# Attention's steps written out as one order of their own for each unit

## The chip, the cores and the metric

The kernel runs on one core of a Trainium2 chip. Its engines are TensorE (PE, matrix products), VectorE (DVE), ScalarE (ACT), GpSimd (POOL) and SyncE (SP), which here issues most DMAs. Each works through its own instructions in the order in which they were issued, and waits on semaphores for the others. The metric is the device time of one execution in microseconds.

## What is computed

A transformer block with adaptive layer norm: attention with a compressive memory over four segments of 512 rows, 32 heads of 18, then a SwiGLU feed-forward part.

```python
def _A_ref(x, wq, wk, wv, wo, beta):
    q, k, v = ...                              # (B, H, N=4, L=512, Dh=18)
    for s in range(N):
        logits = einsum("bhqd,bhkd->bhqk", q[:, :, s], k[:, :, s]) * scale + mask
        a_dot = softmax(logits) @ v[:, :, s]
        pq = phi(q[:, :, s])                   # phi(t) = t + 1 if t > 0 else exp(t)
        a_mem = (pq @ M) / (pq @ z + 1e-6)
        o[s] = g * a_mem + (1 - g) * a_dot     # g = sigmoid(beta)
        pk = phi(k[:, :, s]);  M = M + pk.T @ v[:, :, s];  z = z + pk.sum()
    return o @ wo
...
h = layernorm(x) * (1 + ca) + sa;  x = x + ga * A(h)
h = layernorm(x) * (1 + cb) + sb;  x = x + gb * ((silu(h @ w_gate) * (h @ w_up)) @ w_down)
```

## The kernel before

Three parts follow each other: the projections of segments 0 to 2 (up to some 217 us), attention, and the feed-forward part, whose products are formed by a Strassen-like scheme from sums of blocks of the normed rows (`y`). The change is in attention alone.

Attention is cut into 32 **units**: unit u is segment u // 8 and four heads. In a unit, 12 **score steps** `a` are taken. One score step issues, on PE, the products for one PSUM bank of two kinds and what follows them: for unit u + 2 the logits by rows, `p1_step` (L175), from which DVE takes the row maxima (`junk`, L190); for unit u the logits by columns with the maxima taken off, `p2_step` (L662), from which ACT makes the exponentials `Pt` (L668); POOL then masks the diagonal part (L672). Each kind has three banks. Widths go down from 512 to 128 columns within a unit. Between score steps stand the other steps, each a letter in a table; a digit is a quarter, half or block:

- `V`: the products of unit u - 1's `Pt` with v (`av`, L685, 32 matmuls); `E`: ACT copies them out (L697); `c`: PE transposes them (L706, four matmuls); `d`: DVE divides by the row sums and scales (L714, L715, L722), and POOL adds to the output rows (L723)
- `m`: PE transposes unit u + 1's row maxima (L205); `n`: ACT copies them (L209) and SP sends them by two DMAs into the operand `qs` (L164), where unit u + 1's column products need them
- `M`, `X`: a part of the output projection of an earlier segment (L785, 14 matmuls in four quarters M0 to M3) and the sum with x on DVE (L790); in units 1 to 7 it is segment 3's v projection (L862) instead. `R`, `S`, `T` prepare its left operand: PE transposes, ACT copy, DVE remainder (L759, L765, L769); `Z`, `z` the same for its last columns
- `A`, `B`, `C`, `D`, `G`: the memory part, on PE (L921), ACT, POOL, DVE and POOL; `f`, `h`: loads of phi(q) for it (`pq`, L909), with a POOL memset
- `P`, `Q`, `q`, `Y`: load of a block of wo (L1037), multiply on POOL (L1041), cast on ACT (L1043), remainder on DVE (L1045)
- `l`, `p`, `x`: layer norm of finished rows on DVE, POOL, ACT, with a store; `W`: segment 3's q and k projection, in unit 0

From unit 17 on, two helpers (`stage_a`, `stage_b`) also prepare the feed-forward operands `y`: a load, PE transposes, ACT scaling, then for each operand an ACT cast, a DVE remainder and a store, with POOL differences in between.

The order is that of the Python code (`tc.manual_schedule`). It is set by the table `PAT`: five patterns of 11 places, one for unit 0 and four chosen by the half of the segment and the parity of u, so units with the same pattern have the same order. Next unit's loads (`load_unit(u + 3)`) come at a unit's start, a segment's v loads after place 5, and the `y` steps at places worked out from `KP` and collected in `sched`.

```python
PAT = (("a a Q D", "a G V0123 m E q", "", "a a", "a M0 M1", "n a a c Y M2 d M3 X", "", "a a", "h f a R P Z S T", "", "z a"),
```

Of the kernel before, what the change touches and what calls it, by code (L numbers as in the profile page):

```python
# [42 lines left out]
DS = 4  # L43
DP = (5, 6)
PM = ()
KP = (9, 7, 10, 9)
WW = (11, 15, 18, 22, 27)
SS = (2, 3, 4, 5, 25, 27)
HH = (4, 6, 8, 16, 20, 24)
# [8 lines left out]
WQ = (1, 3, 4, 5, 6)  # L58
E1 = 3
E2 = 2  # L60
PAT = (("a a Q D", "a G V0123 m E q", "", "a a", "a M0 M1", "n a a c Y M2 d M3 X", "", "a a", "h f a R P Z S T", "", "z a"),
# [4 lines left out]
LNA = 1  # L66
S3 = (4, 5, 6, 7, 8, 0, 1, 2, 3)
S1B, S2B, XB = 3, 3, 2
# [8 lines left out]
def block(ctx: ExitStack, tc: tile.TileContext, x, wqk, wv, wo, beta, wgu, wd, c, w_mod, wm01, out):  # L77
# [652 lines left out]
        nc.sync.dma_start(vq[s][:, j, :], vD[s][:, j, :])  # L730

    yt = {}

    def yh(k, kb):
        return yt[1][:, k - 1, kb] if k else yt[0][kb]
# [231 lines left out]
    def event(ev, u):  # L967
        n, a = ev[0], ev[1:]
        s, q = divmod(u, 8)
        if n == "W":  # L970
            seg3_step(int(a))
        elif n == "L":
            load_unit(4)
        elif n == "V":
            for j in a:
                av_step(u - 1, int(j))
        elif n == "E":
            ev_step(u - 1)
        elif n == "m":
            if (NE < u + 1 < NU) or u == 0:  # L980
                mt_a(max(u + 1, NE), ps, *(("x", XB) if u else ("s1", S1B)))
        elif n == "n":
            if (NE < u + 1 < NU) or u == 0:
                mt_b(max(u + 1, NE))
        elif n == "c":
            comb_a(u - 1)
        elif n == "d":
            comb_b(u - 1)
        elif n == "f" and s < 3 and q < 4 and u:
            if u == 1:  # L990
                phi_q(1, 0)
                phi_q(1, 1)
            phi_q(s + 1, q + 1)
        elif n == "h" and s < 3 and q == 0 and u:
            phi_q(s + 1, 0)
        elif n in "DG" and u > 0:
            s1, q1 = divmod(u - 1, 8)
            if n == "G" and u < 9:
                v_st(u - 1)
            if s1 < 3 and q1 >= 4:  # L1000
                (num_d if n == "D" else num_e)(s1 + 1, q1 - 4, fq[-3])
        elif n in "ABC" and s < 3 and 4 <= q < 8:
            if n == "A":
                num_a(s + 1, q - 4, int(a))
            elif n == "B":
                num_b(s + 1, q - 4, int(a))
            else:
                fq[-3] = num_c(s + 1, q - 4)
        elif n in "Zz" and 1 <= s < 4 and q == 0:
            (wo_z if n == "Z" else wo_z2)(s - 1)  # L1010
        elif n in "RST" and 1 <= s < 4 and q % 2 == 0:
            (wo_r if n == "R" else wo_s if n == "S" else wo_t)(s - 1, q // 2)
        elif n in "MX":
            w = u - 9
            if 0 < u < 8:
                if n == "M":
                    v_m(u, int(a))
                else:
                    v_x(u)
            elif w >= 0 and w < 24:  # L1020
                si, h = divmod(w, 2)
                if n == "M":
                    wo_m(si // 4, si % 4, h, int(a))
                else:
                    wo_x(si // 4, si % 4, h)
        elif n in "lpx":
            w = (u - 9) | 1 if u % 2 == 0 else u - 10
            if 0 <= w < 23:
                if n == "l":
                    ln_a(w // 8, w % 8 // 2)  # L1030
                elif n == "p":
                    ln_b()
                else:
                    ln_c()
        elif n == "P" and s == 0 and q in WQ:
            fq[-1] = wk.tile([P, D], F32, tag="woraw", name="woraw", bufs=1)
            nc.sync.dma_start(fq[-1], wo[:, WQ.index(q), :])  # L1037
        elif n in "QqY" and s == 0 and q - 1 in WQ:
            k = WQ.index(q - 1)
            if n == "Q":  # L1040
                nc.gpsimd.tensor_tensor(fq[-1], fq[-1], gaB, op=ALU.mult)  # L1041
            elif n == "q":
                nc.scalar.copy(woh[:, k], fq[-1])  # L1043
            else:
                nc.vector.tensor_tensor(wol[:, k], fq[-1], f32(woh[:, k]), op=ALU.subtract)  # L1045
# [8 lines left out]
    sched = {}  # L1054

    def at(g, f):
        sched.setdefault(g, []).append(f)

    def y_lo(o, kb, f, st, c):
        if kb < 2:  # L1060
# [7 lines left out]
        else:  # L1068
            nc.sync.dma_start(yD[0][o][:96, 4, c], f32(st[:96, 0]))

    def y_part(g, o, kb, f, stf, hv, d=2):
# [7 lines left out]
        at(g, hi)  # L1079
        at(g + 1, lambda: y_lo(o, kb, f, box[0], c))  # L1080
        at(g + 1 + d, lambda: y_store(o, kb, box[0], c))

    def load_cols(dst, s, i0, kh, kb):
        c0 = 288 * kh + 128 * kb
# [13 lines left out]
        for i in range(4):  # L1098
            nc.tensor.transpose(pt[:n, i, :], xb[:, i, :n], ident)

    def step_of(u):
        return 11 * u + KP[u % 8 // 4 * 2 + u % 2]

    def flat(a):
        return a.rearrange("p a b -> p (a b)")

    def stage_a():
# [6 lines left out]
        pts = {}  # L1114
        for i in range(6):
            kb, kh = divmod(i, 2)
            u = 18 + i
            n = P if kb < 2 else 96
            h = yh(kh, kb)
            at(11 * (u - 1) + 1 if i else 11 * u, lambda i=i, kh=kh, kb=kb: load_cols(xb[i % 2], 0, 0, kh, kb))  # L1120
            g = step_of(u) if i else 11 * u + 10
            at(g, lambda i=i, n=n: trans4(xb[i % 2], n, pts, i))
            at(g + 1, lambda i=i, h=h, kh=kh, kb=kb: scaled(h, flat(pts.pop(i)), kh, kb))
            for hv in range(2):
                y_part(g + 2 + 3 * hv, kh, kb, h[:, 256 * hv:256 * hv + 256], lambda j=2 * i + hv: st[j % 4], hv)

    def stage_b():
        big = flat(sk2.tile([P, 5, L], F32, tag="pq", name="yq"))
# [11 lines left out]

        for i in range(6):
            hv, kb = divmod(i, 3)
            u = 25 + i
# [4 lines left out]
            at(11 * (u - 1) + 1, lambda i=i, hv=hv, kb=kb: load(i, hv, kb))  # L1148
            g = step_of(u)

            def trans(i=i, n=n):
                trans4(xb[i % 2], n, pts, i)
# [5 lines left out]

            def sub2(d, x, y_, op=ALU.subtract):
                nc.gpsimd.tensor_tensor(d, x, y_, op=op)  # L1160
            at(g, trans)
            at(g + 1, sc)
            at(g + 2, lambda b=b, h11=h11, a=a, n=n: sub2(b[:n], h11, a[:n]))
            at(g + 3, lambda h00=h00, a=a, n=n: sub2(h00, a[:n], h00))
            y_part(g + 6, 3, kb, h00, lambda i=i: sto[i % 2], hv)
            at(g + 5, lambda h01=h01, h11=h11: sub2(h01, h01, h11))
            at(g + 7, lambda h00=h00, h01=h01: sub2(h01, h01, h00, ALU.add))
            y_part(g + 4, 5, kb, b, lambda i=i: sts[i % 2], hv)

    def y_sum(kb):  # L1170
        n = P if kb < 2 else 96
# [329 lines left out]
    with tc.manual_schedule():  # L1501
# [2 lines left out]
        new_tmp3()  # L1504
        for j in range(4):
            load_v(0, j)
        for u in range(NU + 1):
            s, q = divmod(u, 8)
            if u > 1:
                load_unit(u + 3)  # L1510
            if u == 1:
                while s3q:
                    seg3_step(-1)
# [7 lines left out]
            ma, mb = [], []  # L1521
            ga = chain(*[p2_step(u, j, ma) for j in range(4)])
            gb = p1_seq(u + 2, mb)
            for k in range(11):
                if u == 17 and k == 0:
                    stage_a()
                if u == 24 and k == 0:
                    stage_b()
# [7 lines left out]
                if k == 5 and 4 <= q and s < 3:  # L1536
                    load_v(s + 1, q - 4)
            run(ga)
            run(gb)
        p2.close()  # L1540
        mid.close()
        ps = pool(p2r, "pst", 2, space=PSUM)
# [269 lines left out]
```

## Time and profile before

| | us |
|---|---|
| median of 3 runs | 1844.78 (1842.21 to 1845.96) |
| the profiled execution | 1846.91 |
| its span, first to last instruction | 1844.9 |
| attention's units 1 to 32 and the way to segment 3's output projection, in the span | 232.2 to 565.8 |

The profile's page gives, for one execution, each engine's busy time, and the chain of work that ended last, followed back from the last instruction. The trace behind it can be asked for a stretch of time: busy times by window, what each engine waited for, groups of like instructions, and single instructions in order of time. A matmul's end is modelled in it, so that PE's busy time also covers short holes.

### The profile page before, as it was taken

To read this page: it belongs to the slowest core of one execution; us is meant where nothing else is said; L and a number is where in the kernel's file an instruction comes from. 1 tells how busy PE (TensorE), PEld (TensorE's weight loads), DVE (VectorE), ACT (ScalarE), POOL (GpSimd) and SP (SyncE) were. 2 spreads that over 40 slices of the span, in tenths; PEclk is the share of its full clock that TensorE was granted. 3 is DMA by queue.
4 is the path that set the end of the run, shared out by engine and by line. 5 is a ranking of instruction groups with operands and counts; after the bars stand their busy time and mean duration, and the time that the engine had idled before them with its cause. 6 is when DMAs were issued, how large, how long until landed. Compare 5 with 4: busy or idle time off the path is not lost.

```text
span 1844.9 us, 31121 instructions
## 1 busy us (share of the span) xinstructions
PE 1815.5 (98%) x11061; PEld 1517.1 (82%) x11061; DVE 1491.5 (81%) x3309; ACT 955.7 (52%) x2137; POOL 494.4 (27%) x702
## 2 busy tenths in 40 slices
PE   8999999999999999999999999999999999999999
PEld 5888766666668888888888888888888888888888
DVE  7566578888977888988788898758888888888886
ACT  6444567667775454454445444434544544544541
POOL 2010146455562444446435443300000000000000
PEclk9999999999999999999999999999999999999999
DMA  8677755557648654554464444395333333324331
GB/s 290 234 236 272 244 158 158 159 158 219 175 132 295 227 171 157 191 187 154 153 210 146 147 158 154 122 301 156 123 105 104 102 106 119 102 90 128 105 102 52
DMA packets 178562, 304.49 MB, mean 165 GB/s; under 512 B 25304, under 2 KB 108184, under 8 KB 176616
## 3 DMA queue, kind: packets, MB, share of 16 engines
q1 hardware_dynamic: 151032, 248.66, 43.0%
q10 hardware_dynamic: 27376, 53.86, 8.3%
q8 instruction: 87, 1.43, 0.3%
q14 instruction: 67, 0.55, 0.1%
HBM read 188.42 MB, written 113.33 MB: 164 GB/s over the span
## 4 chain that ended last, share of the span: by engine, by line
PE 89%; DVE 5%; DMA 3%; issue 1%; ACT 1%; SPq 0%; POOL 0%; ACTq 0%; DVEq 0%
PE A L1339 24%; PE pd L1467 13%; PE C L1339 12%; PE pd L1448 10%; PE B L1339 6%; PE pp L524 4%; PE av L685 3%; PE pw L785 3%; PE pv L553 2%; PE s L662 2%; PE s L175 2%; PE pp L809 2%; DVE junk L190 1%; PE pm L513 1%; PE pn L921 1%
## 5 line engine op out<-in xcount | busy, mean ns | idle before, releaser
L1339 PE MATMUL A<-y,wh 128*128 128x512 f32 x1152 | 406.1, 393 | 1.5 <-ACT B L1385 1.0
L190 DVE CUSTOM_DVE_ANT_0 junk<-s,tri 128x384 bf16<-128x384 f32 (+3 forms) x512 | 221.9, 485 | 42.8 <-PE s L175 23.4
L1339 PEld LDWEIGHTS A<-y,wh 128*128 128x128 f32 x1152 | 216.7, 188 | 46.1 <-ACT B L1385 2.5
L1304 DVE TENSOR_TENSOR wl<-O,wh 128x256 fp32r<-128x256 f32 x504 | 248.7, 499 | 2.1 <-ACT wh L1303 1.6
L1339 PE MATMUL A<-y,wl 128*128 128x512 f32 x576 | 226.8, 394 | 0.0
L1453 DVE TENSOR_TENSOR acc<-acc,pd 128x576 f32<-128x576 f32 x216 | 162.0, 751 | 59.4 <-PE pd L1448 51.3
L1339 PE MATMUL C<-y,wh 128*128 128x512 f32 x576 | 203.0, 393 | 0.5 <-DVE cu L1362 0.5
L1303 ACT CAST wh<-O 128x256 fp32r<-128x256 f32 x504 | 197.5, 405 | 3.1 <-DMA yD<-st 3.1
L668 ACT ACTIVATE Pt<-s 128x512 f32<-128x512 f32 (+2 forms) x384 | 179.3, 529 | 35.4 <-PE s L175 22.5
L1467 PE MATMUL pd<-dh,ah 128*128 128x288 f32 x640 | 189.1, 295 | 0.5 <-DVE x L1471 0.5
L1467 PE MATMUL pd<-dh,al 128*128 128x288 f32 x640 | 189.2, 296 | 0.0
L1467 PE MATMUL pd<-dl,ah 128*128 128x288 f32 x640 | 188.9, 295 | 0.0
L1477 DVE TENSOR_TENSOR acc<-acc,pd 128x576 f32<-128x576 f32 x156 | 116.8, 749 | 87.1 <-PE pd L1467 86.6
L1294 POOL TENSOR_TENSOR O<-O 128x384 f32<-128x384 f32 x132 | 148.1, 1136 | 135.2 <-DMA O<-in_wgu_dram 61.7
L1408 ACT CAST ah<-sg 128x512 fp32r<-128x512 f32 x192 | 119.2, 621 | 74.8 <-DVE sg L1363 67.9
L1409 DVE TENSOR_TENSOR al<-sg,ah 128x512 fp32r<-128x512 f32 x192 | 137.2, 714 | 10.9 <-ACT ah L1408 10.8
L1448 PE MATMUL pd<-dh,ah 128*128 128x288 f32 x448 | 133.0, 297 | 0.0
L1448 PE MATMUL pd<-dh,al 128*128 128x288 f32 x448 | 132.5, 296 | 0.0
L1448 PE MATMUL pd<-dl,ah 128*128 128x288 f32 x448 | 132.4, 295 | 0.0
L1467 PEld LDWEIGHTS pd<-dh,ah 128*128 128x128 f32 x640 | 120.8, 189 | 6.8 <-DVE x L1471 0.8
L1467 PEld LDWEIGHTS pd<-dl,ah 128*128 128x128 f32 x640 | 120.5, 188 | 7.1
L1339 PEld LDWEIGHTS C<-y,wh 128*128 128x128 f32 x576 | 108.3, 188 | 21.3 <-DVE cu L1362 1.1
(410 smaller groups left out, 4353.6 us busy)
## 6 DMA issues: line engine op xcount, KB each, us to landing
O<-in_wgu_dram SPq DMA_DIRECT2D x36, 768.0 KB
O<-oD SPq DMA_DIRECT2D x36, 512.0 KB
oD<-O ACTq DMA_DIRECT2D x34, 512.0 KB
ks<-kD SPq DMA_DIRECT2D x64, 216.0 KB
qs<-qD SPq DMA_DIRECT2D x64, 216.0 KB
O<-in_wgu_dram SPq DMA_DIRECT2D x36, 384.0 KB
rD<-wr ACTq DMA_DIRECT2D x36, 336.0 KB
wr<-rD SPq DMA_DIRECT2D x35, 336.0 KB
```

Source lines behind the costliest of these rows:

```text
L190: nc.vector.tensor_tensor_reduce(junk[:, :n], bank[:, n * o:n * o + n], tri[:, L - n:], 1.0, -3e38, op0=ALU.add, op1=ALU.max, accum_out=mx ...
L668: nc.scalar.activation(pt[:, hs[0]:hs[-1] + 1:2, :n], bank[:, :n * per].rearrange("p (a b) -> p a b", a=per), AF.Exp, scale=SCALE)
L1294: eng.tensor_tensor(o[:, d], o[:, a], o[:, b], op=op)
L1303: nc.scalar.copy(wh, o)
L1304: later.append(lambda: nc.vector.tensor_tensor(wl, o, f32(wh), op=ALU.subtract))
L1339: nc.tensor.matmul(bank, lhsT=a, rhs=b, start=(first and n == 0), stop=(n == 6), skip_group_check=not first)
L1408: nc.scalar.copy(ah, src)
L1409: later.append(lambda: nc.vector.tensor_tensor(al, src, f32(ah), op=ALU.subtract))
L1448: nc.tensor.matmul(pd[:, i, :288], lhsT=a[:, tk], rhs=w, start=(k == 0), stop=(k == 2))
L1453: nc.vector.tensor_tensor(o, o, pd[:, :, :288], op=ALU.add)
L1467: nc.tensor.matmul(pd[:, i, :288], lhsT=a[:, tk], rhs=w, start=(k == 0), stop=(k == 5))
L1477: nc.vector.tensor_tensor(o, o, pd[:, :, :288], op=ALU.add)
```

## The change

`PAT`, `KP` and the planner `at`/`sched` go. In their place stands `ORDER`, a table with one line for each unit, in which every step is a token: also the loads of the next stack (`U`), of v (`v0` to `v3`), the start of the two helpers (`SA`, `SB`) and each single `y` step (`y0` to `y131`). A `<` or `>` ahead of a token does the step for the unit before or after, so steps can stand in a neighbour's line. Every step of before is there once; nothing is computed otherwise.

```diff
-PAT = (("a a Q D", "a G V0123 m E q", "", "a a", "a M0 M1", "n a a c Y M2 d M3 X", "", "a a", "h f a R P Z S T", "", "z a"),
...
+ORDER = (
...
+    "a a V0123 a a a G M0 E M1 a a a M2 a a P M3 c X a a >Q d",
...
+    "a a a V0123 <d E a a a m M0 n a a a c <f d M1 a a a M2 M3 R >U X",
...
-        for u in range(NU + 1):
-            s, q = divmod(u, 8)
-            if u > 1:
-                load_unit(u + 3)
...
-            for k in range(11):
...
-                for ev in PAT[q // 4 * 2 + u % 2 if u else 4][k].split():
-                    if ev == "a":
-                        scores(ga, gb, ma, mb)
-                    else:
-                        event(ev, u)
-                for f in sched.pop(11 * u + k, ()):
-                    f()
...
+        def act(tok, u):
+            nonlocal w3, o3, opl_, woh, wol
+            if tok[0] in "<>":
+                act(tok[1:], u + (1 if tok[0] == ">" else -1))
+            elif tok == "a":
+                step_a(u)
+            elif tok == "U":
+                load_unit(u + 3)
...
+            elif tok[0] == "y":
+                parts[int(tok[1:])]()
...
+            else:
+                event(tok, u)
+
+        for u, line in enumerate(ORDER):
+            for tok in line.split():
+                act(tok, u)
```

Three places show what this does to the engines' order. The line numbers of the changed kernel are some 29 higher.

SP, end of unit 0 and unit 1: `kD` is the store of segment 3's k, `pq` the loads of phi(q), `woraw` the load of a block of wo, `vt` a store of segment 3's v. Before:

```order
L288 DMA kD_94<-tmpa 128x2x512
L289 DMA kD_94<-tmpa 128x512
L909 DMA pq_2838<-qF_96 64x512
L909 DMA pq_2838<-qF_96 128x512 x2
L1037 DMA woraw<-in_wo_dram 128x576
```

And now:

```order
L317 DMA kD_94<-tmpa 128x2x512
L318 DMA kD_94<-tmpa 128x512
L901 DMA vD_102<-vt 128x304
L1065 DMA woraw<-in_wo_dram 128x576
L188 DMA ks_987<-kD_91 54x2x512
```

The load of wo has moved ahead of the three phi(q) loads, which follow seven rows later.

DVE, start of unit 10, whose row maxima are those of unit 12 (512 wide at first): PE's `V` of this unit stands behind its third score step, in both orders. Before:

```order
L714 RECIPROCAL r_4359<-px 128x16
L715 TENSOR_TENSOR r_4359<-r_4359,omg 128x16
L722 TENSOR_TENSOR tmp<-px,r_4359 128x288
L190 ISA junk,mx<-s_4373,tri 128x512
L190 ISA mx 128x1
L190 ISA junk,mx<-s_4380,tri 128x512
L190 ISA mx 128x1
L190 ISA junk,mx<-s_4387,tri 128x512
L190 ISA mx 128x1
L190 ISA junk,mx<-s_4415,tri 128x512
```

And now:

```order
L219 ISA junk,mx<-s_4366,tri 128x512
L219 ISA mx 128x1
L219 ISA junk,mx<-s_4373,tri 128x512
L219 ISA mx 128x1
L219 ISA junk,mx<-s_4380,tri 128x512
L219 ISA mx 128x1
L743 RECIPROCAL r_4403<-px 128x16
L744 TENSOR_TENSOR r_4403<-r_4403,omg 128x16
L751 TENSOR_TENSOR tmp<-px,r_4403 128x288
L219 ISA junk,mx<-s_4412,tri 128x512
```

Step d has moved from ahead of the first maximum to behind the third.

PE, the end of attention: `av` is the last unit's V, `pw` the matmuls of M, `px` step c, `pto` the first transposes of segment 3's output projection. Before, from the last score step:

```order
L662 MATMUL s_8614<-qs_2341,ks_2342 128x128 x2
L685 MATMUL av<-Pt,vq_6422 32x512 x4
L685 MATMUL av<-Pt,vq_6422 32x384 x4
L685 MATMUL av<-Pt,vq_6422 32x256 x4
L685 MATMUL av<-Pt,vq_6422 32x128 x4
L785 MATMUL pw<-woh,hh 128x288
```

There, seven `pw` rows stand between `av` and `px`, and seven between `px` and `pto`. Now, from the last of the `pw` rows, all 14 of which stand between the last score step and `av`:

```order
L815 MATMUL pw<-wol,or 128x288
L714 MATMUL av<-Pt,vq_6127 32x512 x4
L714 MATMUL av<-Pt,vq_6127 32x384 x4
L714 MATMUL av<-Pt,vq_6127 32x256 x4
L714 MATMUL av<-Pt,vq_6127 32x128 x4
L735 MATMUL px<-ident,avs 128x128 x4
L789 MATMUL pto<-ident,o_6638 128x128 x4
```

The output projection's last matmuls have moved ahead of the last `av`.

More of the change, by code (lines that the diff above doesn't have):

```diff
@@ L45 @@
 PM = ()
-KP = (9, 7, 10, 9)
 WW = (11, 15, 18, 22, 27)
@@ L732, in block @@
     yt = {}
+    w3 = o3 = opl_ = woh = wol = None
     def yh(k, kb):
@@ L1052, in block @@
     ACT_OP = {1: 0, 2: 1, 3: 2, 4: 6, 5: 3, 6: 4, 7: 5}
-    sched = {}
-    def at(g, f):
-        sched.setdefault(g, []).append(f)
+    parts = []
     def y_lo(o, kb, f, st, c):
@@ L1069, in y_store, with y_part @@
             nc.sync.dma_start(yD[0][o][:96, 4, c], f32(st[:96, 0]))
-    def y_part(g, o, kb, f, stf, hv, d=2):
+    def y_part(o, kb, f, stf, hv):
         n = P if kb < 2 else 96
@@ L1078, in hi @@
             nc.scalar.copy(box[0][:n, 0], f[:n])
-        at(g, hi)
-        at(g + 1, lambda: y_lo(o, kb, f, box[0], c))
-        at(g + 1 + d, lambda: y_store(o, kb, box[0], c))
+        parts.append(hi)
+        parts.append(lambda: y_lo(o, kb, f, box[0], c))
+        parts.append(lambda: y_store(o, kb, box[0], c))
     def load_cols(dst, s, i0, kh, kb):
@@ L1147, in stage_b @@
             a, b = h10[i % 2], t3[i % 2]
-            at(11 * (u - 1) + 1, lambda i=i, hv=hv, kb=kb: load(i, hv, kb))
-            g = step_of(u)
+            parts.append(lambda i=i, hv=hv, kb=kb: load(i, hv, kb))
             def trans(i=i, n=n):
@@ L1160, in sub2 @@
                 nc.gpsimd.tensor_tensor(d, x, y_, op=op)
[L1161 to L1168, printed above, removed]
+            parts.append(trans)
+            parts.append(sc)
+            parts.append(lambda b=b, h11=h11, a=a, n=n: sub2(b[:n], h11, a[:n]))
+            parts.append(lambda h00=h00, a=a, n=n: sub2(h00, a[:n], h00))
+            y_part(3, kb, h00, lambda i=i: sto[i % 2], hv)
+            parts.append(lambda h01=h01, h11=h11: sub2(h01, h01, h11))
+            parts.append(lambda h00=h00, h01=h01: sub2(h01, h01, h00, ALU.add))
+            y_part(5, kb, b, lambda i=i: sts[i % 2], hv)
     def y_sum(kb):
@@ L1506, in block, with step_a @@
             load_v(0, j)
-        for u in range(NU + 1):
-            s, q = divmod(u, 8)
-            if u > 1:
-                load_unit(u + 3)
-            if u == 1:
-                while s3q:
-                    seg3_step(-1)
+        flows = {}
+        def step_a(u):
+            if u not in flows:
+                ma, mb = [], []
+                flows[u] = (chain(*[p2_step(u, j, ma) for j in range(4)]), p1_seq(u + 2, mb), ma, mb)
+            scores(*flows[u])
+        def act(tok, u):
[5 more added lines that the diff above has]
+            elif tok == "U":
+                load_unit(u + 3)
+            elif tok[0] == "v":
+                load_v(u // 8 + 1, int(tok[1]))
+            elif tok == "SA":
+                stage_a()
+            elif tok == "SB":
+                stage_b()
+            elif tok[0] == "y":
+                parts[int(tok[1:])]()
+            elif tok == "O":
                 p2q.close()
@@ L1520, in block @@
                 ot[0] = opl_.tile([P, 4, D], F32, tag="o0", name="o0")
-            ma, mb = [], []
-            ga = chain(*[p2_step(u, j, ma) for j in range(4)])
-            gb = p1_seq(u + 2, mb)
-            for k in range(11):
[L1525 to L1528, printed above, removed]
-                for ev in PAT[q // 4 * 2 + u % 2 if u else 4][k].split():
-                    if ev == "a":
-                        scores(ga, gb, ma, mb)
-                    else:
-                        event(ev, u)
-                for f in sched.pop(11 * u + k, ()):
-                    f()
[L1536 to L1539, printed above, removed]
+            else:
[3 more added lines that the diff above has]
+                act(tok, u)
         p2.close()
```

16 lines of the change are left out of this document (5 added, 11 removed), and 35 rows, old and new, of tables (ORDER, PAT).

## The prediction

> **What bounds the kernel now.** I read the page first: busy shares and the chain that ended last. Then I asked the trace for the stages of attention by window, for what VectorE (DVE) waits for in the middle stage, and for the chain at the places where the order changes.
>
> ```profile
> PE 1815.5 (98%) x11061; PEld 1517.1 (82%) x11061; DVE 1491.5 (81%) x3309; ACT 955.7 (52%) x2137; POOL 494.4 (27%) x702
> ...
> PE 89%; DVE 5%; DMA 3%; issue 1%; ACT 1%; SPq 0%; POOL 0%; ACTq 0%; DVEq 0%
> ```
>
> By these two lines PE bounds everything. But they average over the projections, attention and the feed-forward part, and the change touches attention alone. So the stages matter:
>
> ```profile
> core 0: us, PE busy (x) PEld busy (x) DVE busy (x) ACT busy (x) POOL busy (x), PEclk, DMA share, GB/s
> 232.20:254.60 22.40, 20.78 (x172) 12.52 (x172) 16.19 (x72) 13.91 (x32) 8.74 (x20) 0.92 0.57 172
> 254.60:531.10 276.50, 269.24 (x2375) 179.99 (x2373) 243.21 (x1026) 201.64 (x458) 154.00 (x325) 1.00 0.61 170
> 531.10:565.80 34.70, 30.23 (x239) 20.09 (x238) 16.85 (x52) 21.90 (x50) 22.38 (x34) 0.92 0.43 143
> 565.80:1844.90 1279.10, 1273.32 (x6960) 1119.16 (x6959) 1070.55 (x1807) 604.71 (x1393) 280.95 (x260) 1.00 0.46 148
> ```
>
> Stage I is units 1 and 2, stage II units 3 to 28, stage III the last units and the way into segment 3's output projection. The last row, 69% of the span, is code that the diff leaves alone. In stage II DVE is busy 243.21 of 276.50 us (88%) and idle 33.3. PE's 97% is made of modelled ends, and its weight loads fill 179.99 us (65%); ACT and POOL have 27% and 44% free. I take DVE as the engine that limits stage II, with PE as what it waits for:
>
> ```profile
> DVE junk L190 <- PE s L175: 16.7, 24, 3.6
> DVE junk L190 <- PE s L662: 11.5, 19, 1.0
> DVE r L945 <- POOL r L941: 2.4, 6, 0.6
> ```
>
> The first two rows are 28.2 us; one wait of 3.6 among them ends at 254.55 and belongs to stage I. That leaves **24.6 us** in which the maxima (L190) stand still because PE is doing something other than scores. This is what the change can win in stage II.
>
> The Trainium skill, Perfetto Trace Analysis, section Identifying the Most-Contended Engine, says that matmul busy time is no good measure of how close TensorE is to its limit, and that the weight-load share should be taken. By it PE has a third of stage II free and the sum below stands; read by matmul busy time, PE would be full and the middle term would be nothing, which is my first rival.
>
> **The change, term a: the stall at unit 1.** No work is added or removed; each step is only issued elsewhere.
>
> ```profile
> 230.48 4.70 DMA kD<-tmpa
> 235.26 0.52 SPq L909
> 236.45 1.27 SPq L909
> 237.76 3.76 DMA woraw<-in_wo_dram
> 241.59 1.43 POOL woraw L1041
> 243.05 0.67 ACT woh L1043
> ```
> ```profile
> 254.55 0.69 DVE L190 CUSTOM_DVE_ANT_0 junk<-s,tri 128x512 bf16<-128x512 f32 x1 [3.60 <-PE s L175]
> ```
>
> The phi(q) loads (L909) write memory that segment 3's stores still read, so SP waits 4.70 us for that store, and the woraw load stands behind them. POOL, then ACT's cast, then the exponentials behind it run late, and DVE ends up idle 3.60 us. In the new order the woraw load is ahead of the phi(q) loads, so it no longer waits for the store, and the multiply (Q) follows only at the end of unit 1, the cast (q) after four score steps of unit 2. What is late next is the ordinary DVE rate: stage I idles 22.40 - 16.19 = 6.2 us, and at stage II's 12% it would idle 2.7. I take **3.5 us**; bounds 0 (the load is late anyway) and 6.2.
>
> **Term b: the middle units.** One place shows the mechanism, unit 10:
>
> ```profile
> 323.29 0.25 DVE L714 RECIPROCAL r<-px 128x16 f32<-128x16 f32 x1
> 323.80 0.46 DVE L722 TENSOR_TENSOR tmp<-px,r 128x288 f32<-128x288 f32 x1
> 324.17 0.68 DVE L190 CUSTOM_DVE_ANT_0 junk<-s,tri 128x512 bf16<-128x512 f32 x1
> 324.33 2.36 PE L685 MATMUL av<-Pt,vq 128*32 128x512 f32 x32
> 327.38 0.69 DVE L190 CUSTOM_DVE_ANT_0 junk<-s,tri 128x512 bf16<-128x512 f32 x1 [1.29 <-PE s L175]
> ```
>
> While PE does the 32 av matmuls, DVE eats the three banks of scores that stand ready and then idles 1.29 us. The 0.88 us of step d (323.29 to 324.17) lie before that. In the new order d stands behind the third maximum, inside the hole; 0.4 us of it would be left.
>
> To size this over units 3 to 28 I went through both orders and, for each stretch between two score steps, took PE's time for the steps there, less DVE's time for the steps there, less 1.5 us of scores in hand (two 512-wide maxima), counting only what is above zero. The prices:
>
> ```profile
> 260.91 2.29 PE av L685 x32
> 263.20 0.21 PE pmt L205
> 264.20 2.04 PE pw L862 x14
> 266.79 0.94 PE pn L921 x6
> ```
> ```profile
> L190 DVE CUSTOM_DVE_ANT_0 junk<-s,tri 128x512 bf16<-128x512 f32 x106 | 69.1, 681 | 17.2 <-PE s L662 8.1 <-PE s L175 7.7 <-POOL mc L196 1.0
> L190 DVE CUSTOM_DVE_ANT_0 junk<-s,tri 128x384 bf16<-128x384 f32 x106 | 54.4, 553 | 8.3 <-PE s L175 7.6 <-PE s L662 0.3
> L790 DVE TENSOR_TENSOR xr<-pw,xr 128x288 f32<-128x288 f32 x20 | 9.0, 450 | 0.0
> L881 DVE BATCH_NORM_STATS2 st<-xr 128x6 f32<-128x288 f32 x20 | 8.2, 449 | 0.0
> L769 DVE TENSOR_TENSOR hl<-pto,hh 128x512 fp32r<-128x512 f32 x11 | 7.6, 687 | 0.0
> ```
>
> So V with m is 2.5 us of PE, one M 0.51, A0 0.94, four transposes 0.45; on DVE d is 0.88, X 0.45, T 0.69, and l two of L881 and some small ones. The shortfall comes to 25.1 us in the order before and 12.0 in the new one: of the 26 places with V, 13 had no DVE step beside them before, and now 4 have none. That 25.1 is so near the measured 24.6 is partly luck, for the count puts 21.3 at V, while the rows put 17.2 - 3.6 = 13.6 before 512-wide maxima and most of the rest before 384-wide ones. So I trust the ratio, about a half. Term b is **12 us**; bounds 0 and 24.6. A shorter unit also needs its loads earlier; the DMA queues are busy 61% of the stage, which covers it.
>
> Steps that wait for each other are moved apart as well: R, S, T (PE, ACT, DVE) stood in one place in all 12 units that have them and now no T is beside its R. In stage II these waits hit ACT and POOL, which have room, so I count nothing for them.
>
> **Term c: the end of attention.**
>
> ```profile
> 546.39 3.99 PE av L685 x32
> 557.60 1.01 PE L685 MATMUL av<-Pt,vq 128*32 128x256 f32 x16 [1.05 <-POOL Pt L672]
> 559.74 0.45 PE px L706 x4
> 563.19 0.67 PE L759 MATMUL pto<-ident,o 128*128 128x128 f32 x3 [2.08 <-DVE xr L790]
> ```
>
> The unit-31 av block takes 3.99 us instead of 2.29 (the mean granted clock of the stage is 0.92): 1.7 us lost after PE idled. The last av waits 1.05 us for selects; step d of unit 31, whose POOL add stood ahead of the last select, now follows the last score step. The last output-projection steps (M, X) move ahead of the last av into that wait, so that c follows it without the 1.1 us of seven M matmuls, and X no longer stands between d and the next transposes. Of 1.7 + 1.05 + 2.08 = 4.8 us and the M's 1.1, I take **4 us**: ACT has its exponentials to do whatever the order. Bounds 0 and 7.
>
> **Sum.** 3.5 + 12 + 4 = 19.5 us off the profiled execution's 1846.91 gives 1827.4. The median of the runs is 2.1 below that execution, so the forecast is **1825 us**. All lower bounds give 1845, all upper ones 1807.
>
> **Rivals.** (1) PE is the real limit of stage II, or the holes only move: every DVE step put beside V is missing where it stood, and three score banks stay three. For it speaks PE's 97%; against it the 1.29 us hole that ends on PE with DVE work lying just before it. Then only a and c are won: 1845 - 7.5 = 1837. The same skill page, section Optimization Strategy, warns that a gap which repeats on the engine that should be saturated can mean too few buffers, and no order mends that; by it the time would also be 1837. The trace agrees that the gap repeats (43 waits in two rows), and no run here has another number of banks.
>
> (2) New waits take all of it: a DVE step in a hole waits for its own producer, such as d for its transposes. Then the time stays at 1845.
>
> (3) Slower: the bias row arrives late. Step n sends it through two small DMAs, and the next unit's first exponent product (L662) on PE needs it.
>
> ```profile
> 274.78 6.74 DMA qs<-mr
> ```
> ```profile
> 309.75 1.29 SPq L164 DMA_DIRECT2D qs<-mr  x2
> 312.62 0.55 PE L662 MATMUL s<-qs,ks 56*128 56x128 f32 x2
> PE s L662 <- DMA qs<-mr: 0.5, 2, 0.3
> ```
>
> With six score steps left behind n the next unit followed 312.62 - 309.75 = 2.9 us later; a landing can take 6.74. Before, 7 units have six steps or fewer left; now 15, units 14 and 28 only four. At worst 6.74 - 2.9 = 3.8 us in 8 more units is 31 us: 1825 + 31 = 1856. It decides from about 3 us each. Against it: PE waited for this DMA 0.5 us in all, and the short units have M and A steps behind n that give 1 to 4 us more.
>
> **How the numbers follow.** What a measurement here can tell from no change is about 0.2%, 3.7 us. Forecast (1813 to 1834): 0.55. Rival 1 (1834 to 1841): 0.20. Rival 2 (1841 to 1848.5): 0.10. Rival 3 (over 1848.5): 0.11. Better than 1813: 0.04. Hence faster 0.79, same 0.10, slower 0.11. The range 1811 to 1848 reaches over the first three cases and leaves out rival 3 and the far end of the gains.
>
> **What would show it.** a: no DVE wait over 1 us at unit 2, and the granted clock of stage I at 1.00. b: DVE's wait for PE scores in the middle units at 10 to 16 us, with DVE's busy time unchanged near 243. c: the last units shorter by 3 to 5 us, the last av without a wait for POOL. Everything behind the output projection must take the same time as before. I am wrong if DVE's waits for scores stay above 20 us (rival 1), if waits for POOL or ACT grow by what they lose (rival 2), or if PE's wait for the bias row grows to several microseconds (rival 3).

## The result and the profile after

| | before | after | ratio, 95% interval |
|---|---|---|---|
| first comparison (4 executions each), median us | 1845.1 | 1829.18 (1827.69 to 1833.31) | 0.992, 0.990 to 0.994 |
| second comparison (17 and 6 executions), median us | 1846.08 | 1835.56 (1828.24 to 1840.07) | 0.9943, 0.9923 to 0.9962 |
| profiled execution, us | 1846.91 | 1828.63 | |

The change makes the kernel faster, by 10 to 16 us. The forecast was 1825 us with a range of 1811 to 1848; both medians lie inside, above the forecast. That alone says little: the range also takes in rival 1 and all but the last half microsecond of rival 2, and the second median, 1835.56, lies in the stretch (1834 to 1841) that the prediction gave to rival 1. The page of the changed kernel, the two lines shown of before (busy time of the engines; the chain that ended last):

```profile
PE 1802.9 (99%) x11061; PEld 1514.3 (83%) x11061; DVE 1490.4 (82%) x3309; ACT 953.8 (52%) x2137; POOL 492.6 (27%) x702
...
PE 92%; DMA 3%; DVE 3%; issue 1%; ACT 1%; SPq 0%; ACTq 0%; DVEq 0%
```

No engine does less work or more. PE's share of the chain rose from 89% to 92%, and DVE's fell from 5% to 3%: the chain leaves PE less often. Units 4 to 28 lie between the first exponent products of units 4 and 29. By window (us; busy time and instructions of each engine; granted clock; DMA share and GB/s), before and then after:

```profile
259.94:525.53 265.59, 258.33 (x2278) 172.74 (x2278) 232.64 (x984) 192.77 (x437) 147.74 (x311) 1.00 0.62 173
```

```profile
256.46:510.35 253.89, 249.65 (x2278) 171.02 (x2278) 232.20 (x986) 192.59 (x439) 143.81 (x310) 1.00 0.61 177
```

The same work takes 11.7 us less. What DVE, and then PE, waited for in the changed kernel (total, times, longest):

```profile
DVE junk L219 <- PE s L204: 6.9, 13, 1.2
DVE junk L219 <- PE s L691: 6.5, 12, 1.0
```

```profile
PE s L691 <- DMA qs<-mr: 3.0, 4, 1.0
PE pto L789 <- DVE tmp L751: 1.9, 1, 1.9
PE px L735 <- ACT avs L726: 0.8, 1, 0.8
```

DVE's waits for scores in the middle are 13.4 us, after 24.6; PE's waits for the bias row are 3.0 us, after 0.5. Three starts of work, in the span of each profiled execution, show where the gain arose:

| first PE product of | before | after | difference |
|---|---|---|---|
| unit 4's exponents | 259.94 | 256.46 | -3.48 |
| unit 29's exponents | 525.53 | 510.35 | -15.18 |
| end of the last exponents | 554.91 | 536.49 | -18.42 |

After that nothing changes (-18.1 at the end of the span). By this table the prediction's three terms came out at 3.5, 11.7 and 3.2 us, beside 3.5, 12 and 4. That agreement is misleading, as the experiments show, because the profiled execution of before held something that I had not taken out of it. These are three windows of that execution:

```profile
249.46:252.87 3.41, 3.41 (x18) 1.04 (x22) 1.49 (x8) 0.76 (x2) 0.98 (x4) 0.50 0.56 173
546.42:549.83 3.41, 3.41 (x24) 1.09 (x28) 0.42 (x3) 2.24 (x5) 1.64 (x4) 0.50 0.23 82
563.48:566.89 3.41, 3.41 (x18) 3.27 (x17) 1.78 (x3) 2.18 (x5) 3.16 (x4) 0.50 0.95 341
```

In each, the granted clock of PE is 0.50; I call that a half-clock period. The changed kernel's profiled execution has one such period ahead of the feed-forward part, at 545.76. Whether such a period falls differs between executions, also of one kernel (the changed kernel's second profiled execution has them at 150.63, 451.00 and 546.58). Where it can fall is less free, as the last section shows.

### The profile page after: what moved, and what is told of

It is laid out like the page before. It is cut to its first block, busy times and chain, and to the rows that moved or that the text cites. A ratio compares the mean times of both kernels' runs of the same rounds, so it can differ in the third digit from the quotient of the medians.

```text
span 1826.8 us, 31122 instructions
## 1 busy us (share of the span) xinstructions
PE 1802.9 (99%) x11061; PEld 1514.3 (83%) x11061; DVE 1490.4 (82%) x3309; ACT 953.8 (52%) x2137; POOL 492.6 (27%) x702
## 4 chain that ended last, share of the span: by engine, by line
PE 92%; DMA 3%; DVE 3%; issue 1%; ACT 1%; SPq 0%; ACTq 0%; DVEq 0%
PE A L1357 24%; PE pd L1485 13%; PE C L1357 12%; PE pd L1466 10%; PE B L1357 6%; PE pp L553 4%; PE av L714 4%; PE pw L815 3%; PE s L691 3%; PE s L204 3%; PE pv L582 2%; PE pp L839 2%; DMA y<-yD 1%; DMA qs<-mr 1%; PE pw L892 1%; PE pn L951 1%
## 5 line engine op out<-in xcount | busy, mean ns | idle before, releaser
L697 ACT ACTIVATE Pt<-s 128x512 f32<-128x512 f32 (+2 forms) x384 | 179.4, 528 | 31.6 <-PE s L691 18.1
```

Source lines behind the costliest of these rows:

```text
L697: nc.scalar.activation(pt[:, hs[0]:hs[-1] + 1:2, :n], bank[:, :n * per].rearrange("p (a b) -> p a b", a=per), AF.Exp, scale=SCALE)
```

## The experiments

**Which part of the new order is worth what.** Three kernels each take one stretch of units in the new order and the rest in that of before (steps that cross a border are done once); a fourth undoes the end alone. Each diff shows the first lines that differ from the changed kernel.

```diff
 units 3 and on as before (front alone)
-    "a a U a M0 m n P G a <f a M1 a a M2 a >Q a a M3 a a c X",
+    "<f U a a m n a a a M0 M1 a a a M2 a a M3 X f a a c d P G",
...
 units 0 to 2 and 29 to 32 as before (middle alone)
-    "a a V0123 a a a G M0 E M1 a a a M2 a a P M3 c X a a >Q d",
+    "O a a V0123 E a a a M0 M1 a a a M2 a a M3 X f a a c d P G",
...
```

> Units 0 to 2 (and with them unit 3's V and E) in the new order, everything behind in the order of before. Theory, each term of the sum stands alone: unit 4 begins 3.5 us earlier than in the profile of before, no DVE wait over 1 us before a maximum of unit 2, and all of the 3.5 us is kept to the end: 3 to 4.5 us faster (ratio 0.998). Rival, the later order takes the stall back (the same loads are late one unit on): unit 4 no earlier or the gain gone by unit 10, within 1 us of before.

> Units 3 to 28 in the new order, units 0 to 2 and 29 to 32 as before. Theory: the stall of 3.6 us at unit 2 stays, from unit 4 to unit 29 11 to 12.5 us are won, DVE's waits for PE scores there fall from 24.6 to about 13 us: 10.5 to 13 us faster (ratio 0.994). Rival, PE is the limit of the middle and the gain seen there came from the head start at unit 1: 0 to 4 us faster (ratio 0.998 to 1).

The kernel with the new end alone has the lines of before in units 0 to 28.

> Units 29 to 32 in the new order, everything ahead of them as before. Theory: the last scores end 1 to 2.5 us earlier and the way from them to the output projection is shorter by the rest: 3 to 4.5 us faster (ratio 0.998); the 31st unit's av at the full clock, about 2.3 us. Rival, the end is set by ACT's exponentials whatever the order, and the gain at the end of the whole change came from units ahead of it: within 1.5 us of before.

```diff
 units 29 to 32 as before (end undone)
-    "a y53 <T y74 a a V0123 E l p m n a y119 a a x M0 c a d M1 M2 a a a M3 X y101 a a y79 y98 y96 y107 y108",
+    "y53 y79 y74 y87 <T a a y96 y119 l a V0123 p m n a a a M0 y103 E M1 y101 y104 a a a y98 M2 M3 c X x y99 y102 y105 d a a a y100 y107 y108",
...
```

> Units 0 to 28 in the new order, units 29 to 32 as before: the new end alone undone. Theory, the end is worth nothing (as the new end alone was) and the front and the middle are worth more together than the 2.2 and 7.4 us that each gave alone: within 2 us of the changed kernel, ratio 0.991 to 0.993. Rival, the end pays once the middle is in order: 4 to 7 us slower than the changed kernel, ratio 0.994 to 0.996.

The first three stand beside a median of 1843.65 us for before, the last beside 1846.08, so the ratios are what can be compared.

| new order in | median us | ratio to before | 95% interval |
|---|---|---|---|
| units 0 to 2 | 1841.42 | 0.9986 | 0.9973 to 0.9998 |
| units 3 to 28 | 1836.23 | 0.9964 | 0.9951 to 0.9977 |
| units 29 to 32 | 1844.43 | 1.0001 | 0.9991 to 1.0011 |
| units 0 to 28 | 1832.70 | 0.9931 | 0.9917 to 0.9945 |

The front is worth about 2 us and the end nothing. The middle gives 7 us alone. With the front it and the front give 13 us, as much as the whole change within the intervals. The middle alone lost part of its gain to one thing, which its trace shows as PE's waits in units 4 to 28:

```profile
PE s L691 <- DMA qs<-mr: 4.3, 3, 2.7
PE s L204 <- DMA qs<-qD: 0.7, 1, 0.7
```

From unit 4 to unit 20 it is as fast as the changed kernel (157.9 and 158.2 us). At the start of unit 23 PE waits 2.7 us for the bias row, and a half-clock period follows at 451.88. So the new middle has little to spare at the DMA queues there, and a small shift in time decides whether that shows.

The kernel with the new end alone is also a second look at the order of before in units 0 to 28, without a half-clock period there:

```profile
256.63:521.83 265.20, 257.75 (x2278) 172.71 (x2277) 232.42 (x984) 192.72 (x437) 147.73 (x311) 1.00 0.62 174
```

Against it the middle wins 265.20 - 253.89 = 11.3 us. Two more traces of the new middle without a half-clock period there took 254.64 us (the end undone) and 255.77 (the last kernel below), and the old middle behind the new front 264.51, so that at the full clock the middle wins 8.7 to 11.3 us. From unit 0's first exponents to unit 4's it takes 60.07 us (196.56 to 256.63) and the changed kernel 58.38 (198.08 to 256.46): the front wins 1.7 us at the full clock.

**The changed kernel once more**, unaltered, beside the end undone and two kernels below.

> The changed kernel again, beside the kernels below, for more executions of it. Theory, the half-clock periods that fall differently in each execution make up 2 to 3 us of the 15.9 us shown so far: executions with a mean granted clock of 0.999 or more lie near 1828 us, against 1842 us for those of the kernel before, a ratio of 0.992 to 0.993. Rival, the whole difference is there at the full clock too: 1826 us or less for those executions.

Over the three comparisons in this study the executions of before with a mean granted clock of 0.999 or more have a median of 1842.28 us (20 of 51), and those at 0.997 or less 1847.30 (21). For the changed kernel, in both comparisons, it is 1828.24 (3 of 10) and 1837.39 (5). So near the full clock the change is worth 14.0 us, as my first expectation had it (a mean of 0.999 can still hold one such period: the changed kernel's first profiled execution has one and is among the three). But the changed kernel loses as much to half-clock periods as before, or more, and not 2 to 3 us less.

**Is the middle won by DVE work in V's hole?** My mechanism was that DVE steps beside V fill the time in which PE gives DVE no scores. One kernel adds only that to the order of before (six d, eleven T), and one takes it out of the new order.

```diff
 order of before, units 8 to 10
-    "U a a D a G V0123 m E a a a n a a c d a a h f a R Z S T z a",
-    "U a a V0123 m n E a a a M0 M1 a a a M2 a a M3 X f a a c d",
-    "U a a a V0123 m E a a a M0 M1 n a a c M2 d M3 X a a f a R S T a",
+    "U a a D a G V0123 m E a a a n a a c d a a h f a R Z S z a",
+    "U a a V0123 <T m n E a a a M0 M1 a a a M2 a a M3 X f a a c",
+    "U a a a V0123 <d m E a a a M0 M1 n a a c M2 d M3 X a a f a R S a",
...
```

> The order of before with one thing changed: in units 9 to 29 the six steps d and eleven steps T that stood at the end of a unit follow the next unit's V. Theory, DVE work in the hole is the gain of the middle: DVE's waits for PE scores fall from about 30 us (units 1 to 29 of the order before) to 24 or less, units 9 to 29 take 207 to 209 us instead of 212.4 (the new order: 204.9), 3 to 6 us faster than before (ratio 0.997 to 0.998). Rival, these steps are missing where they stood: 0 to 1 us.

```diff
 changed order, units 10 and 11
-    "a a a V0123 <d E a a a m M0 n a a a c <f d M1 a a a M2 M3 R >U X",
-    "a a <S a V0123 <T l m n a a a M0 M1 a p a <f E M2 a a a M3 c X a",
+    "a a a V0123 E a <d a a m M0 n a a a c <f d M1 a a a M2 M3 R >U X",
+    "a a <S a V0123 a <T l m n a a M0 M1 a p a <f E M2 a a a M3 c X a",
...
```

> The changed kernel with the DVE steps that stand beside V in units 9 to 28 (d, T, l and y remainders, 20 of them in 15 units) put behind the next score step, out of the time in which PE does V. Theory, DVE work in that hole is what won the middle: DVE's waits for PE scores there rise from 13 us to 18 us or more, 5 to 9 us slower than the changed kernel (ratio 0.994 to 0.997). Rival, PE is the limit and DVE's waits cost nothing: within 2 us of the changed kernel.

The first is not faster but slower: 1857.69 us, ratio 1.0072 (1.0053 to 1.0091). The second is slower by more than I gave it: 1849.90 us, ratio 1.0016 (1.0003 to 1.0028), 14 us above the changed kernel beside it. DVE's waits for scores did not follow the first expectation: in the first kernel, from unit 9 to 28, they rose to 24.6 us from 17.2 in the order of before. In the second they rose as expected, to 23.8 us from 7.8 in the changed kernel. What PE waited for from unit 9 on, in the first and in the second:

```profile
PE av L714 <- POOL mc L228: 2.8, 2, 1.4
PE pmt L234 <- DVE hl L799: 2.2, 2, 1.1
...
PE av L714 <- DVE hl L799: 1.9, 1, 1.9
```

```profile
PE pmt L234 <- ACT avs L726: 2.2, 5, 0.8
PE pw L815 <- DVE tmp L751: 2.2, 2, 1.4
PE pw L815 <- DVE hl L799: 1.8, 3, 1.0
```

Those for `hl` (step T) and `tmp` (step d) are waits for the two PSUM banks that V, c, m, M, A and R share, which these steps have still to read, or in M for the operand that T makes. None of these rows is in the changed kernel's trace. (In the second kernel, m also stands one score step later in units 9, 11, 21 and 22, and n in three of them; and its profiled execution lost time to a half-clock period of 13.65 us at 253.13, ahead of all the moved steps.) So a DVE step cannot be priced by where DVE has a hole: it has to be done before PE needs what it holds, and the new order meets that with R, S and T in neighbouring units and M, X and A apart. That the new order wins by this is argued, not shown: both kernels put new waits in, so neither measures the hole by itself.

**Which engine limits the middle?** The changed kernel with less work for DVE:

```diff
-                nc.vector.tensor_tensor_reduce(junk[:, :n], bank[:, n * o:n * o + n], tri[:, L - n:],
+                w = n // 2 if a is None else n
+                nc.vector.tensor_tensor_reduce(junk[:, :w], bank[:, n * o:n * o + w], tri[:, L - n:L - n + w],
```

> The changed kernel with the row maxima of units 2 to 31 taken over the first half of each tile's columns only, some 0.28 us less of DVE for each of the 512-wide tiles. Theory, DVE limits the middle: units 4 to 28 (253.9 us) become shorter by 15 us or more, 15 to 30 us faster than the changed kernel (ratio 0.975 to 0.985). Rival, PE is the limit: within 4 us of the changed kernel.

It took 1830.83 us, ratio 0.9926 (0.9908 to 0.9943): no gain. Units 9 to 17, which no half-clock period touched, by window: before, changed, and with less DVE work.

```profile
312.73:406.49 93.76, 92.58 (x812) 61.02 (x811) 81.76 (x353) 64.87 (x146) 47.88 (x105) 1.00 0.53 160
```

```profile
305.41:394.10 88.69, 88.36 (x811) 59.92 (x811) 81.44 (x350) 64.10 (x145) 47.01 (x105) 1.00 0.57 167
```

```profile
303.25:390.79 87.54, 87.27 (x811) 59.67 (x811) 58.94 (x347) 63.87 (x145) 47.03 (x105) 1.00 0.57 170
```

DVE's busy time (the third busy time) falls by 22.5 us and the window by 1.15 us, while DVE's waits for scores grow from 4.5 to 19.4 us in it:

```profile
DVE junk L220 <- PE s L204: 12.5, 17, 1.4
DVE junk L220 <- PE s L692: 6.9, 11, 1.1
```

In the new order these waits cost nothing. PE is its limit, and 87.5 us is about what PE needs for these units. (Over all of units 4 to 28 this kernel took 256.07 us against 253.89, with a wait of 2.7 us for the bias row and a half-clock period at 449.17, both in unit 23.) The order of before needed 6.2 us more, and the new one 1.2. Most of those 5 us stand in no wait row, since a matmul's modelled end runs on until the next one starts. They show when for each kind of matmul the times from its start to the next start are summed; a wait of a matmul is then counted in the row of the one ahead of it. Units 4 to 27, the order of before (from the trace with the new end alone) and the changed kernel, in us:

```
matmul                      before    after
s<-ks,qs (for the maxima)    46.45    40.46
s<-qs,ks (exponents)         47.65    49.28
both kinds of scores         94.10    89.74
pn (A)                       20.53    17.88
px (c)                       14.66    12.70
pto (R)                       7.17     5.45
all                         253.78   243.42
```

PE loses 4.4 us less behind scores and 6.3 us less behind pn, px and pto, which stand among the steps that share two banks. The two kinds of scores take turns, and what is counted with which is not stable (the kernel with the end undone has 42.23 and 48.36), so only their sum is read.

Was it DVE's reading that PE waited for at the scores? PE may write a bank for the maxima again when DVE has read it. For the 384 matmuls of that kind in units 4 to 27 the traces show how long after DVE's last signal to it each one started. One value stands out, 0.04 to 0.05 us: 45 starts in the order of before (the same trace), 16 in the changed kernel (20 and 21 with the end undone and with U early) and 1 with less DVE work, while no other hundredth of a microsecond from 0 to 0.4 holds more than 9. These are starts that DVE let go. So in the order of before DVE's reading did hold PE up, about 45 times, and in the new one less than half as often. What share of the gain this makes is not shown, and for pn, px and pto the cause is argued from the order alone. The order of before with less DVE work, which would price it, was not run.

**Too few buffers?** The kernel before with the banks divided otherwise:

```diff
-S1B, S2B, XB = 3, 3, 2
+S1B, S2B, XB = 4, 2, 2
```

> The kernel before, in its own order, with four PSUM banks for the scores that give the maxima and two for those that give the exponentials, instead of three and three. Rule, a gap that repeats means too few buffers: DVE's waits for the scores of the maxima (20.1 us from unit 1 on) fall below 12 us and it is 4 to 10 us faster (ratio 0.995 to 0.998). My theory, a bank more does not fill the hole, since PE is at V and the third bank is seldom empty when DVE asks, and a bank less makes PE wait for ACT: within 3 us or slower.

1908.43 us, ratio 1.0345 (1.0321 to 1.0369). PE's first wait in attention:

```profile
PE s L662 <- ACT Pt L668: 41.2, 88, 1.2
```

PE now waits 88 times for ACT's exponentials to free a bank. A fourth bank for the maxima does not pay for a third one of the exponents, so of these two divisions that of before is the better. More banks in all were not tried.

**The bias row and the loads.** The row's step n earlier in the four units where PE waited for it:

```diff
-    "a a a D V0123 <P E G m Q a a a M0 M1 a U n a a q M2 M3 v2 X Y A0 B0 a a a A1 c P B1 d C",
+    "a a a D V0123 <P E G m Q a n a a M0 M1 a U a a q M2 M3 v2 X Y A0 B0 a a a A1 c P B1 d C",
...
-    "a y45 a y36 a V0123 E <C m y30 D U a y25 n a a M0 M1 M2 y31 M3 y33 X c G d a a a A0 B0 A1 y34 B1 a a y37 R y38 a",
+    "a y45 a y36 a V0123 E <C m y30 D a n y25 U a a M0 M1 M2 y31 M3 y33 X c G d a a a A0 B0 A1 y34 B1 a a y37 R y38 a",
...
```

> The changed kernel with step n (the bias row) moved two to four score steps ahead in units 6, 19, 22 and 27, behind which PE waited 0.4, 1.0, 0.9 and 0.7 us for it (3.0 us together). Theory, those waits lie on the path: they go, and it is 2 to 3 us faster than the changed kernel (18 to 19 us faster than before, ratio 0.990). Rival, DVE is behind at these places anyway and PE has time to wait: within 1 us of the changed kernel (ratio 0.991 to 0.992).

1851.39 us, ratio 1.0039 (1.0025 to 1.0052): the gain of the change is lost, and more. PE's waits in attention, and three windows:

```profile
PE s L204 <- DMA qs<-qD: 12.8, 3, 4.8
PE s L691 <- DMA qs<-mr: 2.6, 1, 2.6
```

```profile
290.56:297.39 6.83, 5.52 (x33) 2.24 (x37) 2.19 (x7) 1.08 (x2) 1.41 (x1) 0.50 0.60 173
461.23:468.06 6.83, 6.23 (x38) 2.41 (x38) 3.61 (x11) 1.20 (x3) 0.55 (x1) 0.50 0.61 212
519.26:526.09 6.83, 4.75 (x25) 1.91 (x29) 3.23 (x10) 1.38 (x3) 1.59 (x2) 0.50 0.61 180
```

To bring n forward I had put the next stack's loads (U) behind it in units 6, 22 and 27, and it is these that now arrive late, three times by over 4 us on average; after each, the clock is halved for 6.83 us. So both the bias row and the stack's loads are due just in time in the new order. The opposite move, U early:

```diff
-    "a a U a <C Q V0123 m n a a a E M0 <v0 M1 D a a a v1 c M2 d G q M3 X a a a A0 B0 A1 B1 C Y",
+    "U a a a <C Q V0123 m n a a a E M0 <v0 M1 D a a a v1 c M2 d G q M3 X a a a A0 B0 A1 B1 C Y",
...
```

> The changed kernel with the loads of the next stack (U) at the start of units 4 to 28, as before the change, up to seven score steps earlier, all else as changed. Theory, the bias row lands late because the stack's loads lie just ahead of it in the queues: PE's wait for it (3.0 us in four places) falls below 1 us, 2 to 4 us faster than the changed kernel (ratio 0.989 to 0.991). Rival, the early loads hold up SP or meet other transfers: within 1 us of it or slower.

1830.72 us, ratio 0.9924 (0.9909 to 0.9940). PE's waits in units 4 to 28 begin with these rows:

```profile
PE pt L1124 <- DMA yh<-xh: 1.6, 1, 1.6
...
PE s L691 <- DMA qs<-mr: 0.5, 1, 0.5
```

The wait for the bias row falls from 3.0 to 0.5 us, as expected, and a load of the feed-forward operands is late in its place. The time is not clearly another than that of the changed kernel. The last kernel took what had looked good together: U early, the late load (and one behind it) moved, and the end of before.

```diff
-    "a <S a a <T V0123 m U <C E y21 l a p a a M0 y27 n M1 x v1 y14 M2 D y22 y23 M3 X a G a a c A0 d B0 a a a y28 y29 y24 A1 B1",
+    "U a <S a a <T V0123 m <C E y21 l a p a a M0 y27 n M1 x v1 y14 M2 D y22 y23 M3 X a G a y36 a c A0 d B0 a a a y28 y29 y24 A1 B1",
...
```

> The changed kernel's front and middle, with the stack's loads (U) at the start of units 4 to 28, the two loads of y in units 21 and 22 (y36, y45) moved half a unit, and units 29 to 32 as before. Theory, these were the places at which PE stood idle for 1 us or more and the clock was then halved in some executions: PE's waits for DMAs below 1.5 us in all, no half-clock period in attention, median 1827 to 1830 (ratio 0.990 to 0.992) with a spread of executions under 6 us. Rival, the half-clock periods come from elsewhere: 1831 to 1835 with the spread of the changed kernel (12 us).

1832.25 us, ratio 0.9929 (0.9915 to 0.9944). Its executions lie within 8 us (1828.82 to 1836.61), nearer together than the changed kernel's 12, but over the 6 us that I had given; and it is no faster. Unit 23 has no wait for a DMA and no half-clock period here; the profiled execution has one of 6.83 us at 532.94, behind a window with only 0.65 us of shown PE idle time. No kernel here is shown to beat the change.

## Why the prediction held, and where its reasons did not

**What bounds stage II: wrong.** "I take DVE as the engine that limits stage II" does not hold in the new order, where the kernel that halves the width of DVE's row maxima gains nothing. For the order of before it was not tried; there units 9 to 17 took 93.8 us, of which PE needed about 87.5 and DVE was busy for 81.8. So PE's 97% was closer to the truth. The rule of the Trainium skill that I leaned on (Perfetto Trace Analysis, section Identifying the Most-Contended Engine: not matmul busy time but the weight-load share, beside which the page names the share of peak FLOPs) led away from it here: with weight loads at 59.92 of 88.69 us (68%) PE had 1.2 us to give. The first rival had the engine right and its consequence wrong. PE was the limit, yet 9 to 11 us could be won, because PE itself lost that time inside its modelled busy time, by the sums of starts in part to banks that DVE had still to read.

**Term b: right size, wrong price.** 12 us forecast, 11.7 between the two profiled executions, 8.7 to 11.3 over the traces at the full clock, and DVE's waits at 13.4 us within the 10 to 16 that I had given. But I priced the gain by DVE's waits, and these are no price: 19.4 us of them cost nothing with less DVE work, and the DVE steps put beside V alone cost 12 us. So the near hit was in part luck. In place of "which DVE step stands beside V" the traces put how soon a bank that PE wants is free. The sentence that the queues, busy 61% of the stage, cover the earlier loads was wrong as well: PE's waits for the bias row rose to 3.0 us.

**Term a: mis-sized.** Forecast 3.5, measured 2.2 us alone (0.4 to 5 by the interval) and 1.7 in traces at the full clock. The 3.48 us of the profiles include the half-clock period at 249.46, and so did the wait that the term was priced by. In the order of before without that period (the trace with the new end alone) it is not 3.60 us but 1.99:

```profile
251.23 0.69 DVE L219 CUSTOM_DVE_ANT_0 junk<-s,tri 128x512 bf16<-128x512 f32 x1 [1.99 <-PE s L204]
```

No DVE wait at unit 2 is over 1 us, and the clock of the stage is 1.00, as I had asked for; but the second also holds for the order of before, when no half-clock period falls there.

**Term c: wrong.** Forecast 4, measured 0 (within 2 us). 1.7 us of it were taken straight from a half-clock period of one execution (the av block of 3.99 us). The moved steps do what they should, and the last av waits for nothing; but the wait goes elsewhere:

```profile
541.60 0.66 PE L735 MATMUL px<-ident,avs 128*128 128x128 f32 x4 [0.76 <-ACT avs L726]
544.13 0.52 PE L789 MATMUL pto<-ident,o 128*128 128x128 f32 x3 [1.88 <-DVE tmp L751]
545.16 0.30 PE L789 MATMUL pto<-ident,o 128*128 128x128 f32 x1 [0.51 <-DVE o L752]
```

With M and X gone from behind it, c has nothing to cover ACT's copy, nor the next transposes DVE's division. Right behind these waits, at 545.76, comes the half-clock period. From unit 29 to the feed-forward part the traces show 51.7 us for the new end without such a period (one trace), 52.8 to 54.3 with one (six), and 52.9 to 53.8 for the old end without (three; a fourth, with DVE steps moved, 54.6). So by that one trace the moved steps win 1 to 2 us, and the half-clock period that mostly follows takes that back.

**The sum.** 19.5 forecast, 18.3 between the two profiled executions, 14.0 near the full clock, 10 to 16 by the medians. It came near because term b, the large one, had nearly the right size; the other two were half-clock periods for the most part. Taking 2.1 us off for the median of the runs was not enough: the profiled execution was slower than those near the full clock by 1846.91 - 1842.28 = 4.6 us, with its three half-clock periods ahead of the feed-forward part.

**The rivals.** The second (new waits eat all) did not happen in the changed kernel, but did in both kernels that moved DVE steps alone. The third did happen on a small scale (PE's wait for the bias row from 0.5 to 3.0 us), and small shifts in time made it larger: 4.3 us in the middle alone, and with the loads behind it 15.4 us when n was moved.

## What to carry to other kernels

Where one engine feeds another through few banks, the sums of starts to next starts of the feeding engine show what it loses, and its starts right behind the fed engine's signals show to whom; the waits of the fed engine don't. Before a wait is priced from one profiled execution, look at the granted clock in the stretch itself: whether a half-clock period falls there can change from one execution to the next, though the order decides where one can fall. And when steps with DMAs are moved, look at the loads that they change places with: a load that comes late can be paid a second time, when the clock is halved behind it.

## What the runs showed of the hardware

PE's granted clock went to 0.50 for 3.41 us, twice that or, in one trace, four times that, behind stretches in which PE stood idle for a part of the time. The Trainium skill (TensorE: Matmul & The Clock Gate, Part 1) gives 3413 ns as the length of the window by which the clock is gated, and the traces agree on the length. By its table an idle window of that length halves the clock; here no whole idle window was needed. In the 3.41 us just ahead, the traces show 1.2 to 3.3 us of PE idle time in most cases, but 0.64 to 0.84 us in five; and on the grid of these periods other windows with 1.4 to 1.7 us were followed by the full clock. The modelled ends hide part of the idle time, so that no bound can be read here.

These periods come back at the same places. At unit 23 five of the nine traces with the new middle have one: the five in which PE waited 1.4 to 3.4 us for a DMA there, and none of the four with 0.9 us or less. Of the seven traces with the new end, six have one 6.8 to 9.3 us behind the last exponents, around PE's waits for the copy E and the division d; the seventh has the same waits and no period. In the feed-forward part two traces have one, both 673 us behind the last exponents (at 1216 us with the new middle alone, at 1211 with the end undone), behind a DMA wait of 1.8 and 2.1 us.

The executions of the kernel before run from 1841 to 1849 us, the longer ones at the lower mean clock; that spread is more than half as large as the whole effect of the change.
